# Gated linear attention and two MLPs on one core: plain float32 prefix sums, a state split by head, a guard behind the exponential, twelve weight pieces converted early

## The chip, the cores and the metric

The kernel runs on one core of a Trainium2 chip. TensorE (PE, its weight loads shown as PEld), VectorE (DVE), ScalarE (ACT) and GpSimd (POOL) each work through a queue of their own in program order, and SyncE (SP) issues every DMA. The metric is the device time of one execution in microseconds (us). Lower is better.

## The reference

For 4 batches of 8 heads, 768 tokens and a head size of 48, a gated linear attention runs over the tokens, with a forget gate for each of the 48 rows of the state:

```python
f = 1.0 / (1.0 + np.exp(-f_logit))
for t in range(S):
    state = f[:, :, t, :, None] * state + np.einsum('bhd,bhe->bhde', k[:, :, t], v[:, :, t])
    y[:, :, t] = np.einsum('bhd,bhde->bhe', q[:, :, t], state)
```

Its output x (768 tokens by 384 channels per batch) goes through a token mixing of rank 32 and an MLP, then through a second MLP with a convolution of width 3 over the tokens and a gate:

```python
u = x + (x.T @ U @ V).T
x = u + np.maximum(u @ w_ch1, 0) @ w_ch2          # 384 -> 1536 -> 384
h = np.maximum(x @ w_in, 0)                       # 384 -> 1024
c = conv3(h, conv_w)
out = (h / (1 + np.exp(-c))) @ w_out              # 1024 -> 384
```

The weights arrive as float64, and the kernel turns them into float32 itself.

## The kernel before

**Attention in chunks.** The 768 tokens of a batch are cut into 6 chunks of 128, 24 chunks in all, done one after the other by a loop over `i` (L786 to L858). With the running sum n of log(1 + exp(-f_logit)) inside a chunk, q is scaled by exp(-n) and k by exp(n); then the chunk's own part is a masked product of the two, and what comes from earlier chunks is q times a state of 48 x 48 per head. For chunk g the steps are, by the names in the code:

- `gate_max` (L436, tile sp): the lowest logit is cut off, on POOL from chunk 4 on. `gates` (L441): ACT takes exp (L443) and ln (L444) of sp. From chunk 3 on the result is then split in two float32r parts, the high one sph by ACT (L451), the rest spl by POOL (`sub`, L70).
- `prefix` (L455): the running sum is a matmul with a triangle of ones, once for each part, into the PSUM tile n. ACT makes a = exp(-n) (L467), POOL q times a (tile qh, L473). DVE cuts n off at 64 into b (L470), ACT takes exp of b (L476), POOL multiplies k by it (tile kh, L477).
- `ends` and `ends_back` (L500, L503): the last row of a goes to DRAM and comes back as a column, tile ga. `decay` (L507): POOL multiplies a block mask by it (gm, L510).
- `transposes` (L518) of qh and kh on PE, copied by ACT; `scores` (L527), 8 matmuls into two banks s; `mask` (L537), two multiplications by the triangle on DVE, tiles p.
- `state` (L544): k times v for a pair of heads at a time, 4 matmuls of 112 x 96 into bank kv, off-diagonal blocks included; DVE adds the state (wtmp, L558) and multiplies by gm (w, L559), which clears those blocks too.
- `out_chunk` (L581): y from w and qT and from p and v, in 32-column strips that share the array; `out_evac` (L594) copies it into u; `tokens` (L597), `mix_in` (L609), `mix_z` (L619) and `mix_out` (L635) do the token mixing.

Iteration i runs the scores and output of chunk i, the prefix of chunk i+2 and the gates of chunk i+4. Loads are issued on SP two to three iterations ahead into three buffers per tensor, and each waits for the buffer's last reader.

**Weights.** w_ch1 and w_ch2 come in 24 pieces of 384 KB; DVE turns a piece into float32 with five operations (`w64_steps`, L112 to L116), ACT and POOL split it into float32r parts (`split`, L88). N_EARLY = 6 pieces (three pairs, w1 and w2) are converted inside the attention loop, `SLOT` = 3 steps per iteration put ahead of the masks (`slot`, L743). The other 18 are converted two per unit of the first MLP.

**MLPs.** From iteration 22 on `mlps` is advanced. A unit of the first MLP is 18 float32r matmuls up and 18 down, 384 columns each; there are 12 units for each batch, and DVE makes the low part rl of each unit's activations (L200) in the same queue as the conversions.

Of the kernel before, what the change touches and what calls it, by code (L numbers as in the profile page):

```python
# [17 lines left out]
N_EARLY = 6  # L18
SLOT = 3
N_WHOLE = 3  # L20
# [4 lines left out]
EXP_LIMIT = 64.0  # L25
LEAST_NORMAL = float(897 << 20)
# [3 lines left out]
def kernel(  # L30
# [369 lines left out]
    tri_r = gc.tile([128, 128], F32R, name="tri_r")  # L400
# [3 lines left out]
    bmask = gc.tile([128, 1, D2], F32, name="bmask")  # L404
# [12 lines left out]
    sph, spl, bt = {}, {}, {}  # L417
    gms = {}
# [17 lines left out]
    def gate_max(g):  # L436
        sp = spt[g] = ga2.tile([128, H, D], F32, tag="sp", name="sp")
        (nc.vector if g < 4 else nc.gpsimd).tensor_scalar(  # L438
            out=sp, in0=ft.pop(g), scalar1=LEAST_LOGIT, scalar2=None, op0=ALU.max)

    def gates(g):  # L441
        sp = spt.pop(g)
# [3 lines left out]
        if g < N_WHOLE:  # L446
            sph[g] = sp
            return lambda: None
        h_ = ga2.tile([128, H, D], F32R, tag="sph", name="sph")
        l_ = ga2.tile([128, H, D], F32R, tag="spl", name="spl")  # L450
        nc.scalar.copy(out=h_, in_=sp)  # L451
        sph[g], spl[g] = h_, l_
        return lambda: sub(nc.vector if g < 4 else nc.gpsimd, l_, sp, h_.bitcast(F32))

    def prefix(g, between=None):  # L455
        n = bank(6, [128, DM], "n")
        if g >= N_WHOLE:
            mm(n, tri_r, sph.pop(g).rearrange("p h d -> p (h d)"), True, False)
            mm(n, tri_r, spl.pop(g).rearrange("p h d -> p (h d)"), False, True)
        else:  # L460
            mm(n, tri, sph.pop(g).rearrange("p h d -> p (h d)"), True, True)
# [4 lines left out]
        def up():  # L466
            nc.scalar.activation(out=heads(a_t[g % 3]), in_=nv, func=ACTF.Exp, scale=-1.0)  # L467

        def down():
            nc.vector.tensor_scalar(out=b_, in0=nv, scalar1=EXP_LIMIT, scalar2=None, op0=ALU.min)  # L470

        def q_hat():
            eng.tensor_tensor(out=heads(q_t[g % 2]), in0=qt.pop(g), in1=heads(a_t[g % 3]), op=ALU.mult)  # L473
# [5 lines left out]
        if g < 3:  # L479
            down()  # L480
            up()
            nc.scalar.activation(out=b_, in_=b_, func=ACTF.Exp)
            if between:
                between()
            q_hat()
            eng.tensor_tensor(out=heads(k_t[g % 3]), in0=kt.pop(g), in1=b_, op=ALU.mult)
            return None, None
        up()
        q_hat()
        return down, k_hat  # L490

# [15 lines left out]
    def decay(g):  # L507
        if (g + 1) % NCH:
            gm = wk1.tile([MP, NP, D2], F32, tag="gm", name="gm")
            nc.gpsimd.tensor_tensor(  # L510
                out=gm, in0=bmask[0:MP].to_broadcast([MP, NP, D2]),
                in1=ga[0:MP, g, :].unsqueeze(2).to_broadcast([MP, NP, D2]), op=ALU.mult,
            )
            gms[g] = gm

    qT, kT, sc, pt, wt = {}, {}, {}, {}, {}
# [26 lines left out]

    def state(g):  # L544
        if (g + 1) % NCH == 0:
            return lambda: None
        kh, vv = k_t[g % 3], vt[g]
        ps = bank(7, [MP, NP, D2], "kv")
        for p in range(NP):
            vp = vv[:, p * 128:p * 128 + 2 * VO].rearrange("p (j x) -> p j x", j=2)[:, :, 0:D]  # L550
            mm(ps[:, p, :], kh[:, p, 0:MP], vp, True, True)

        def rest():
            w = wk2.tile([MP, NP, D2], F32, tag="w", name="w")
            gm = gms.pop(g)
            if g % NCH:
                tmp = wk1.tile([MP, NP, D2], F32, tag="wtmp", name="wtmp")
                nc.vector.tensor_tensor(out=tmp, in0=ps, in1=wt[g], op=ALU.add)  # L558
                nc.vector.tensor_tensor(out=w, in0=tmp, in1=gm, op=ALU.mult)  # L559
            else:  # L560
                nc.vector.tensor_tensor(out=w, in0=ps, in1=gm, op=ALU.mult)
            wt[g + 1] = w

        return rest
# [3 lines left out]
    def groups(g, ps, parts, first):  # L568
        started = set() if first else set(range(4))
        rounds = [[] for _ in range(4)]  # L570
        for part in parts:
            rounds[part[0] % 4].append(part)
        while any(rounds):
            for q in rounds:
                if q:
                    gr, lhsT, rhs = q.pop(0)
                    m, c = divmod(gr, 4)
                    mm(ps[32 * c:32 * (c + 1), m, :], lhsT, rhs, c not in started, False)
                    started.add(c)

    def out_chunk(g):  # L581
        yt[g] = ps = bank(4, [128, KD, C], "y")
        qq, vv, pp = qT.pop(g), vt.pop(g), pt.pop(g)
        parts = []
        if g % NCH:
            w = wt.pop(g)
            parts += [(3 * p + x, w[:, p, 32 * x:32 * (x + 1)], qq[:, p, :]) for p in range(NP) for x in range(3)]
        for x, gr, j in ((0, 0, 0), (1, 1, 0), (2, 1, 1), (3, 2, 1)):
            parts += [(3 * p + gr, vv[:, 128 * p + 32 * x:128 * p + 32 * (x + 1)], pp[j][:, p, :]) for p in range(NP)]
        groups(g, ps, parts, True)  # L590
# [28 lines left out]
    def mix_z(b):  # L619
        z = zps.pop(b)  # L620
        lo = wk1.tile([R, DM], F32, tag="zt", name="zt")
        zz = wk1.tile([R, DM], F32, tag="zz", name="zz")
        st = wk1.tile([3 * R, DM], F32R, tag="zst", name="zst")
        nc.scalar.copy(out=lo, in_=z[R:2 * R])
        nc.vector.tensor_tensor(out=zz, in0=z[0:R], in1=lo, op=ALU.add)
# [49 lines left out]
    with tc.manual_schedule():  # L675
# [6 lines left out]
        nc.gpsimd.memset(bmask, 1.0)  # L682
        nc.gpsimd.affine_select(
            out=bmask[:, 0, 0:D], in_=bmask[:, 0, 0:D], pattern=[[0, D]], base=D - 1,
            channel_multiplier=-1, compare_op=ALU.is_ge, fill=0.0,
        )
        nc.gpsimd.affine_select(
            out=bmask[:, 0, D:D2], in_=bmask[:, 0, D:D2], pattern=[[0, D]], base=-64,
            channel_multiplier=1, compare_op=ALU.is_ge, fill=0.0,
        )  # L690
# [5 lines left out]
        nc.vector.tensor_copy(out=tri_r, in_=tri)  # L696
        for t in v_t:
            nc.gpsimd.memset(t[:, 0:NP * 128].rearrange("p (a x) -> p a x", a=NP)[:, :, D:VO], 0.0)
        for t, x in ((q_t[1], 0.0), (k_t[1], 0.0), (a_t[1], 1.0), (k_t[2], 0.0), (a_t[2], 1.0)):
            nc.gpsimd.memset(t, x)  # L700
# [9 lines left out]
        prefix(0, lambda: gate_max(1))  # L710
        warm(WARM_UP[1])
        gate_low = gates(1)
        transposes(0)
        gate_low()
# [58 lines left out]
        slot(5)
        gate_low()
# [10 lines left out]
        lows = []  # L785
        for i in range(1, NG):  # L786
            for g in ((i + 3,) if i == 1 else (5, 6) if i == 2 else (i + 4,)):
                if g < NG:
                    load(kt, k, "k", g)
                    load(qt, q, "q", g)  # L790
            for g in ((5, 6) if i == 1 else (i + 5,)):
                if g < NG:
                    load(ft, f_logit, "f", g)
# [4 lines left out]
            if i > 1:  # L798
                decay(i)
            for low in lows:  # L800
                low()
            lows.clear()
# [13 lines left out]
            if down:  # L816
                down()
# [3 lines left out]
            if i == 1:  # L821
                decay(1)
            state(i)()
# [4 lines left out]
            for g in ((i + 3,) if i == 1 else (5, 6) if i == 2 else (i + 4,)):  # L828
                if g < NG:
                    gate_max(g)  # L830
                    lows.append(gates(g))
            if i == 1:
                lows.pop()()
# [8 lines left out]
            elif (i - 1) % NCH > 1:  # L842
                for at in (1, 7) if i % 2 else (1,):
# [195 lines left out]
```

## Time and profile before

| what | before |
|---|---|
| median of 3 runs | 700.9 us (700.42 to 701.51) |
| the profiled execution, its own time | 703.99 us |
| its span, first to last instruction | 702.3 us |
| granted TensorE clock over the span | 0.987 |
| busy, share of the span: PE, DVE, ACT, POOL | 94%, 66%, 41%, 26% |
| first matmul of the first MLP | at 182.1 us |
| chain that ended last: PE, DVE, POOL, DMA | 66%, 11%, 7%, 5% |

The busy shares are averages over two stages: until 182 us the attention, where four engines and the DMA queues take turns, and after it the MLPs, where PE hardly pauses. A matmul record overlaps the next, so a busy PE of 94% is no measure of its speed; the distance from start to start is. Parts of the text below call the distance between the scores of two successive chunks an interval.

### The profile page before, as it was taken

Reading aid. Unit: us, or ns where it says so; the run is one execution under the profiler, and the core shown is the slowest. Engines: PE = TensorE matmul, PEld = TensorE weight load, DVE = VectorE, ACT = ScalarE, POOL = GpSimd, SP = SyncE. Lnnn points to the kernel's source line nnn. Section 1 sums busy time; section 2 is a strip of 40 time slices with the busy share of each in tenths; the row PEclk is TensorE's granted clock in tenths of the full one; section 3 lists DMA queues with packets and bytes.
Section 4 is the critical chain, followed back from the end, with each engine's and each line's share of the span. In section 5 each row is a group of like instructions: output and inputs, shape, how many; then the busy total and the mean of one; then the engine's idle time right before and its main releaser. Section 6 shows DMA issues by size and latency. Waiting matters only on the chain.

```text
span 702.3 us, 12589 instructions
## 1 busy us (share of the span) xinstructions
PE 657.2 (94%) x5084; PEld 626.8 (89%) x5084; DVE 460.5 (66%) x717; ACT 290.5 (41%) x571; POOL 185.2 (26%) x189
## 2 busy tenths in 40 slices
PE   7788798888999999999999999999999999999994
PEld 6676677777898989999999999999999999999994
DVE  5756786867699999666911141113898769769762
ACT  5567676676422232222311131113454544544532
POOL 4667777784133341111300020002002002002000
PEclk9989999999999999999999999999999999999998
DMA  9868576751033322222000000000000100100102
GB/s 175 160 122 158 116 154 141 151 98 50 2 112 113 113 91 68 68 68 68 23 0 1 1 1 1 0 1 1 1 1 0 69 1 1 67 1 1 69 0 73
DMA packets 126919, 41.13 MB, mean 59 GB/s; under 512 B 113300, under 2 KB 124076, under 8 KB 126852
## 3 DMA queue, kind: packets, MB, share of 16 engines
q1 hardware_dynamic: 126852, 40.24, 24.5%
q8 instruction: 42, 0.69, 0.4%
q14 instruction: 25, 0.20, 0.1%
HBM read 35.46 MB, written 4.77 MB: 57 GB/s over the span
## 4 chain that ended last, share of the span: by engine, by line
PE 66%; DVE 11%; POOL 7%; DMA 5%; issue 4%; ACT 4%; SPq 1%; POOLq 0%; DVEq 0%; ACTq 0%
PE a L67 31%; PE b L67 30%; POOL sp L438 2%; POOL kh L477 2%; DVE cvt L112 2%; DVE cvt L113 2%; DVE cvt L114 1%; DMA f<-in_f_logit_dram 1%; DVE cvg L116 1%; DVE cvg L115 1%; POOL spl L70 1%; PE y L67 1%; DVE ul L70 1%; POOL qh L473 1%; DMA ga<-ends_d 1%
## 5 line engine op out<-in xcount | busy, mean ns | idle before, releaser
L196 ACT ACTIVATE rh<-a 128x384 fp32r<-128x384 f32 x96 | 47.3, 492 | 211.1 <-PE a L67 211.1
L200 DVE SCALAR_TENSOR_TENSOR rl<-a,rh 128x384 fp32r<-128x384 f32 x96 | 52.1, 555 | 123.9 <-ACT rh L196 123.6
L70 POOL TENSOR_TENSOR ul<-u,uh 128x384 fp32r<-128x384 f32 x24 | 29.4, 1253 | 281.7 <-ACT uh L89 272.2
L67 PE MATMUL a<-uh,w1h 128*128 128x384 f32 x288 | 97.0, 337 | 3.3 <-ACT w2h L89 3.3
L67 PE MATMUL a<-ul,w1h 128*128 128x384 f32 x288 | 96.7, 336 | 0.0
L67 PE MATMUL b<-rh,w2h 128*128 128x384 f32 x288 | 96.5, 335 | 0.0
L67 PE MATMUL b<-rh,w2l 128*128 128x384 f32 x288 | 96.3, 334 | 0.0
L67 PE MATMUL a<-uh,w1l 128*128 128x384 f32 x288 | 96.3, 334 | 0.0
L67 PE MATMUL b<-rl,w2h 128*128 128x384 f32 x288 | 96.3, 334 | 0.0
L67 PE MATMUL b<-woh,w1h 128*128 128x384 f32 x264 | 70.9, 337 | 0.0
L67 PE MATMUL a<-ul,winh 128*128 128x384 f32 x192 | 65.3, 340 | 2.2 <-DVE ul L70 2.2
L67 PE MATMUL a<-uh,winh 128*128 128x384 f32 x192 | 64.5, 336 | 0.0
L67 PE MATMUL a<-uh,winl 128*128 128x384 f32 x192 | 64.4, 335 | 0.0
L67 PEld LDWEIGHTS a<-uh,w1h 128*128 128x128 f32 x288 | 54.1, 188 | 5.3 <-ACT w2h L89 5.3
L250 ACT ACTIVATE c<-c 128x768 f32<-128x768 f32 x31 | 26.3, 848 | 68.9 <-DVE c L280 68.8
L67 PEld LDWEIGHTS a<-ul,w1h 128*128 128x128 f32 x288 | 54.1, 188 | 0.6 <-DVE ul L70 0.6
L67 PEld LDWEIGHTS b<-rh,w2h 128*128 128x128 f32 x288 | 54.1, 188 | 0.4 <-issue 0.3
L67 PEld LDWEIGHTS b<-rl,w2h 128*128 128x128 f32 x288 | 54.1, 188 | 0.0
L67 PEld LDWEIGHTS a<-uh,w1l 128*128 128x128 f32 x288 | 54.1, 188 | 0.0
L67 PEld LDWEIGHTS b<-rh,w2l 128*128 128x128 f32 x288 | 54.1, 188 | 0.0
L67 PEld LDWEIGHTS b<-woh,w1h 128*128 128x128 f32 x264 | 48.1, 188 | 0.0
L67 PE MATMUL b<-wol,w1h 128*128 128x384 f32 x132 | 44.4, 336 | 0.0
(133 smaller groups left out, 1357.1 us busy)
## 6 DMA issues: line engine op xcount, KB each, us to landing
raw<-in_moe_w_ch_dram SPq DMA_DIRECT2D x24, 384.0 KB
f<-in_f_logit_dram SPq DMA_DIRECT2D x24, 192.0 KB
k<-in_k_dram SPq DMA_DIRECT2D x24, 192.0 KB
q<-in_q_dram SPq DMA_DIRECT2D x24, 192.0 KB
v<-in_v_dram SPq DMA_DIRECT2D x48, 96.0 KB
out_dram<-o SPq DMA_DIRECT2D x24, 192.0 KB
raw<-in_moe_w_in_dram SPq DMA_DIRECT2D x8, 384.0 KB
raw<-in_moe_w_out_dram SPq DMA_DIRECT2D x8, 384.0 KB
```

Source lines behind the costliest of these rows:

```text
L67: nc.tensor.matmul(out=out, lhsT=lhsT, rhs=rhs, start=start, stop=stop, skip_group_check=True)
L70: eng.tensor_tensor(out=out, in0=a, in1=b, op=ALU.subtract)
L112: lambda: ve.tensor_scalar(out=t, in0=hi, scalar1=3, scalar2=0x3FFFFFFF, op0=ALU.logical_shift_left, op1=ALU.bitwise_and),
L113: lambda: ve.scalar_tensor_tensor(out=t, in0=hi, scalar=-(1 << 30), in1=t, op0=ALU.bitwise_and, op1=ALU.bitwise_or),
L114: lambda: ve.scalar_tensor_tensor(out=t, in0=lo, scalar=29, in1=t, op0=ALU.logical_shift_right, op1=ALU.bitwise_or),
L115: lambda: ve.tensor_scalar(out=g, in0=hi, scalar1=0x7FF00000, scalar2=None, op0=ALU.bitwise_and),
L116: lambda: ve.scalar_tensor_tensor(out=w, in0=g, scalar=LEAST_NORMAL, in1=t.bitcast(F32), op0=ALU.is_ge, op1=ALU.mult),
L196: nc.scalar.activation(out=rh[:, hf], in_=ps, func=ACTF.Relu)
L200: nc.vector.scalar_tensor_tensor(out=rl[:, hf], in0=ps, scalar=0.0, in1=rh[:, hf].bitcast(F32), op0=ALU.max, op1=ALU.subtract,)
L250: nc.scalar.activation(out=c, in_=c, func=ACTF.Sigmoid)
L438: (nc.vector if g < 4 else nc.gpsimd).tensor_scalar(out=sp, in0=ft.pop(g), scalar1=LEAST_LOGIT, scalar2=None, op0=ALU.max)
L477: eng.tensor_tensor(out=heads(k_t[g % 3]), in0=kt.pop(g), in1=b_, op=ALU.mult)
```

## The change

- **Prefix sums in plain float32.** The split of sp (L451, L70) is gone, and one float32 matmul with `tri` replaces the two of float32r, for every chunk.
- **Guard behind the exponential.** ACT takes exp(n) straight from PSUM; the cut-off (min and max in one two-operator instruction) is then made on b in SBUF, by POOL from chunk 2 on. DVE's cut-off of n is gone. `gate_max` on POOL also becomes a two-operator instruction, min with 3.0e38 and max with the lowest logit.
- **Block-diagonal state, updated in the next chunk.** k times v is made in strips of 32 rows for each head by itself (16 matmuls of 32 x 48), behind y of the chunk. In the next iteration DVE adds the state (two operations of 48 x 192) and POOL multiplies by ga (two more). gm and the block mask are gone.
- **Order.** From iteration 4 on `gates(i + 3)` stands ahead of the prefix instead of `gates(i + 4)` at the iteration's end, and `gate_max(i + 4)` at its end. Loads of k and q are issued for chunk i+3, of f for i+4.
- **Twelve weight pieces** in the attention, five steps per iteration (3 ahead of the masks, 2 at the end). `mix_z` copies both halves of z out by ACT; `mix_out` uses other banks.

```diff
-N_EARLY = 6
-SLOT = 3
+N_EARLY = 12
+SLOT = (3, 2)
+EARLY_GATES = 4
...
     def gate_max(g):
-        (nc.vector if g < 4 else nc.gpsimd).tensor_scalar(
-            out=sp, in0=ft.pop(g), scalar1=LEAST_LOGIT, scalar2=None, op0=ALU.max)
+        if g < 4:
+            nc.vector.tensor_scalar(out=sp, in0=ft.pop(g), scalar1=LEAST_LOGIT, scalar2=None, op0=ALU.max)
+        else:
+            nc.gpsimd.tensor_scalar(
+                out=sp, in0=ft.pop(g), scalar1=LARGEST, scalar2=LEAST_LOGIT, op0=ALU.min, op1=ALU.max)
...
-            mm(n, tri_r, sph.pop(g).rearrange("p h d -> p (h d)"), True, False)
-            mm(n, tri_r, spl.pop(g).rearrange("p h d -> p (h d)"), False, True)
+        mm(n, tri, sps.pop(g).rearrange("p h d -> p (h d)"), True, True)
...
         def k_hat():
-            nc.scalar.activation(out=b_, in_=b_, func=ACTF.Exp)
+            nc.scalar.activation(out=b_, in_=nv, func=ACTF.Exp)
+            eng.tensor_scalar(
+                out=b_, in0=b_, scalar1=exp(EXP_LIMIT), scalar2=0.0, op0=ALU.min, op1=ALU.max)
             eng.tensor_tensor(out=heads(k_t[g % 3]), in0=kt.pop(g), in1=b_, op=ALU.mult)
...
     def state(g):
...
+        kvs[g] = ps = bank(7, [128, NP, D], "kv")
...
         for p in range(NP):
+            for x in range(4):
+                e = p * 128 + (x // 2) * VO
+                parts.append((x, ps[32 * x:32 * (x + 1), p, :], kh[:, p, 32 * x:32 * (x + 1)], vv[:, e:e + D]))
+    def state_end(g):
...
             if g % NCH:
...
+                nc.vector.tensor_tensor(out=tmp[r], in0=ps[r], in1=w_t[g % 2][r, :, cs], op=ALU.add)
+                nc.gpsimd.tensor_tensor(out=w[r, :, cs], in0=tmp[r], in1=end, op=ALU.mult)
...
             out_evac(i - 1)
             scores(i)
+            if i % NCH:
+                state_end(i - 1)
+            if EARLY_GATES <= i and i + 3 < NG:
+                gates(i + 3)
             follow = slot_end()
             if 1 < i < FILL_FROM:
-                slot(SLOT)
+                slot(SLOT[0])
...
-            state(i)()
...
+            if EARLY_GATES <= i + 1 and i + 4 < NG:
+                gate_max(i + 4)
+            if 1 < i < FILL_FROM:
+                slot(SLOT[1])
```

**POOL, one iteration with a weight piece, before** (spl the low part of the gates, w1l that of a weight piece):

```order
L510 TENSOR_TENSOR gm<-bmask,ga 112x384
L70 TENSOR_TENSOR spl<-sp,sph 128x384
L70 TENSOR_TENSOR w1l<-cvg,w1h 128x3x128
L473 TENSOR_TENSOR qh_113<-q,a_111 128x8x48
L477 TENSOR_TENSOR kh_116<-k,b 128x8x48
L438 TENSOR_SCALAR sp<-f 128x384
```

The same place on POOL in the changed kernel (b is the guard, w_105 the state):

```order
L528 TENSOR_TENSOR w_105<-wtmp,ga 48x4x48 x2
L71 TENSOR_TENSOR w1l<-cvg,w1h 128x3x128
L455 TENSOR_TENSOR qh_113<-q,a_111 128x8x48
L459 TENSOR_SCALAR b<-b 128x384
L461 TENSOR_TENSOR kh_116<-k,b 128x8x48
L440 TENSOR_SCALAR sp<-f 128x384
```

gm and spl have gone, two halves of w and the guard have come; sp still closes the iteration.

**ACT, the same iteration, before**:

```order
L443 ACTIVATE sp<-sp 128x384
L444 ACTIVATE sp<-sp,one 128x384
L451 CAST sph<-sp 128x384
L595 COPY u_68<-y 128x3x128
L89 CAST w1h<-cvg 128x3x128
L467 ACTIVATE a_110<-n 128x8x48
```

ACT in the changed kernel:

```order
L571 COPY u_68<-y 128x3x128
L445 ACTIVATE sp<-sp 128x384
L446 ACTIVATE sp<-sp,one 128x384
L90 CAST w1h<-cvg 128x3x128
L454 ACTIVATE a_110<-n 128x8x48
```

The copy of y, which PE's next transposes wait for, has moved ahead of the gates; the gates' exponential and logarithm still stand ahead of a, which POOL's qh waits for.

**PE, one iteration behind the scores, before**:

```order
L67 MATMUL n<-sph,tri_r 128x384
L67 MATMUL n<-spl,tri_r 128x384
L67 MATMUL z<-xh,uhl 64x384
L67 MATMUL z<-xl,uhl 64x384
L600 MATMUL xt<-ident,u_68 128x128 x3
L67 MATMUL kv<-v_118,kh_115 112x96 x4
L522 MATMUL qTp<-ident,qh_114 112x128 x4
```

PE in the changed kernel, from the same place to the end of the iteration:

```order
L68 MATMUL n<-sp,tri 128x384
L68 MATMUL z<-xh,uhl 64x384
L68 MATMUL z<-xl,uhl 64x384
L576 MATMUL xt<-ident,u_68 128x128 x3
L486 MATMUL qTp<-ident,qh_114 112x128 x4
L486 MATMUL kTp<-ident,kh_117 112x128 x4
L68 MATMUL mix<-vst,zst 128x384
L68 MATMUL y<-qT,w_105 32x128 x12
L68 MATMUL y<-p_1435,v_120 32x128 x8
L68 MATMUL y<-p_1451,v_120 32x128 x8
L68 MATMUL kv<-v_120,kh_116 32x48 x16
```

The prefix is one matmul, and kv has moved from the middle of the iteration to its end.

## Rows read from the trace of the kernel before

**Rows 1.** Stretches (us): PE, PEld, DVE, ACT, POOL busy (count), clock, DMA share, GB/s

```profile
15.68:46.82 31.14, 22.02 (x287) 18.77 (x284) 19.33 (x33) 17.41 (x36) 20.12 (x21) 0.84 0.79 151
46.82:176.36 129.54, 112.41 (x1728) 94.03 (x1724) 97.43 (x167) 89.28 (x184) 93.70 (x90) 0.99 0.62 122
130.68:137.00 6.32, 6.08 (x101) 5.21 (x97) 6.02 (x11) 4.38 (x9) 5.39 (x6) 1.00 0.79 167
170.46:176.36 5.90, 5.66 (x99) 4.84 (x95) 4.43 (x9) 3.27 (x7) 0.00 (x0) 1.00 0.17 65
```

**Rows 2.** Timeline of PE: start, us, scores of chunks 1, 5 and 23

```profile
15.68 1.16 PE L67 MATMUL s<-qT,kT 48*128 48x128 f32 x16
...
52.45 1.16 PE L67 MATMUL s<-qT,kT 48*128 48x128 f32 x16
...
176.36 1.16 PE L67 MATMUL s<-qT,kT 48*128 48x128 f32 x16
```

**Rows 3.** Groups by line and form, 0 to 185 us: busy us, mean ns | idle

```profile
L438 POOL TENSOR_SCALAR sp<-f 128x384 f32<-128x384 f32 x20 | 26.4, 1321 | 0.0
L473 POOL TENSOR_TENSOR qh<-q,a 128x384 f32<-128x384 f32 x22 | 22.3, 1013 | 6.4 <-ACT a L467 5.4 <-POOL spl L70 0.9
L477 POOL TENSOR_TENSOR kh<-k,b 128x384 f32<-128x384 f32 x21 | 21.8, 1038 | 4.9 <-ACT b L476 4.7
L70 POOL TENSOR_TENSOR spl<-sp,sph 128x384 fp32r<-128x384 f32 x20 | 20.0, 1003 | 21.5 <-ACT sph L451 21.5
...
L444 ACT ACTIVATE sp<-sp,one 128x384 f32<-128x384 f32 x24 | 14.8, 616 | 0.8
...
L443 ACT ACTIVATE sp<-sp 128x384 f32<-128x384 f32 x24 | 12.5, 522 | 28.9 <-POOL sp L438 26.2 <-DVE sp L438 2.5
L467 ACT ACTIVATE a<-n 128x384 f32<-128x384 f32 x24 | 11.8, 492 | 9.8 <-PE n L67 6.0 <-DVE b L470 3.8
...
L451 ACT CAST sph<-sp 128x384 fp32r<-128x384 f32 x21 | 10.7, 512 | 0.7
```

**Rows 4.** Waits, 0 to 185 us: us in total, times, longest

```profile
ACT sp L443 <- POOL sp L438: 26.2, 17, 2.5
POOL spl L70 <- ACT sph L451: 21.5, 18, 1.8
POOL gm L510 <- DMA ga<-ends_d: 13.4, 4, 9.6
```

**Rows 5.** Timeline of PE: a plain prefix with its successor, a split one

```profile
13.90 0.84 PE L67 MATMUL n<-sp,tri 128*128 128x384 f32 x2
14.66 1.08 PE L67 MATMUL y<-p,v 128*32 128x128 f32 x32
...
108.31 0.45 PE L67 MATMUL n<-sph,tri_r 128*128 128x384 f32 x1
...
108.76 0.34 PE L67 MATMUL z<-xh,uhl 128*64 128x384 f32 x1
```

**Rows 6.** Other POOL groups by line and form, 0 to 185 us

```profile
L70 POOL TENSOR_TENSOR uhl<-cvg,uhl 128x192 fp32r<-128x192 f32 x1 | 0.6, 598 | 1.9 <-ACT uhl L89 1.9
...
L700 POOL MEMSET kh<- 128x512 f32 x2 | 1.0, 518 | 0.0
```

**Rows 7.** Timeline of DVE: one conversion step beside POOL's w1l, one alone

```profile
117.88 1.24 DVE L114 SCALAR_TENSOR_TENSOR cvt<-raw,cvt 128x384 int32<-128x384 int32 x1
...
193.93 0.56 DVE L114 SCALAR_TENSOR_TENSOR cvt<-raw,cvt 128x384 int32<-128x384 int32 x1
```

**Rows 8.** Chain that ended last: start, us; units with and without conversions

```profile
232.41 0.93 DVE rl L200 x2
...
239.47 0.93 DVE rl L200 x2
...
273.47 3.12 PE a L67 x18
276.59 3.12 PE b L67 x18
```

More of the change, by code (lines that the diff above doesn't have):

```diff
@@ L403 @@
     ends_d = dr.tile([NG, 1, NP * 128], F32, name="ends_d")
-    bmask = gc.tile([128, 1, D2], F32, name="bmask")
+    w_t = [gc.tile([MP, NP, D2], F32, name=f"w{i}") for i in range(2)]
     one = gc.tile([128, 1], F32, name="one")
@@ L416 @@
     ft, qt, kt, vt = {}, {}, {}, {}
-    sph, spl, bt = {}, {}, {}
-    gms = {}
+    sps = {}
     def load(dst, src, nm, g):
@@ L505, in ends_back @@
             nc.sync.dma_start(out=ga[0:MP, g, :], in_=ends_d[g].rearrange("o (p d) -> d (o p)", d=128)[0:MP])
[L507 to L516, printed above, removed]
+    qT, kT, sc, pt = {}, {}, {}, {}
     def transposes(g):
@@ L542, in mask, with strips @@
         pt[g].append(t)
+    kvs = {}
     def state(g):
-        if (g + 1) % NCH == 0:
-            return lambda: None
         kh, vv = k_t[g % 3], vt[g]
-        ps = bank(7, [MP, NP, D2], "kv")
+        kvs[g] = ps = bank(7, [128, NP, D], "kv")
+        parts = []
         for p in range(NP):
[L550 to L555, printed above, removed]
+            for x in range(4):
+                e = p * 128 + (x // 2) * VO
+                parts.append((x, ps[32 * x:32 * (x + 1), p, :], kh[:, p, 32 * x:32 * (x + 1)], vv[:, e:e + D]))
+        return parts
+    def state_end(g):
+        ps, w = kvs.pop(g), w_t[(g + 1) % 2]
+        for j in range(2):
+            r, cs = slice(64 * j, 64 * j + D), slice(j * D, (j + 1) * D)
+            end = ga[r, g, :].unsqueeze(2).to_broadcast([D, NP, D])
             if g % NCH:
-                tmp = wk1.tile([MP, NP, D2], F32, tag="wtmp", name="wtmp")
-                nc.vector.tensor_tensor(out=tmp, in0=ps, in1=wt[g], op=ALU.add)
-                nc.vector.tensor_tensor(out=w, in0=tmp, in1=gm, op=ALU.mult)
-            else:
-                nc.vector.tensor_tensor(out=w, in0=ps, in1=gm, op=ALU.mult)
-            wt[g + 1] = w
-        return rest
+                tmp = wk1.tile([MP, NP, D], F32, tag=f"wtmp{j}", name="wtmp")
+                nc.vector.tensor_tensor(out=tmp[r], in0=ps[r], in1=w_t[g % 2][r, :, cs], op=ALU.add)
+                nc.gpsimd.tensor_tensor(out=w[r, :, cs], in0=tmp[r], in1=end, op=ALU.mult)
+            else:
+                nc.vector.tensor_tensor(out=w[r, :, cs], in0=ps[r], in1=end, op=ALU.mult)
     xh, xl = {}, {}
-    def groups(g, ps, parts, first):
-        started = set() if first else set(range(4))
+    def strips(parts, started):
         rounds = [[] for _ in range(4)]
         for part in parts:
-            rounds[part[0] % 4].append(part)
+            rounds[part[0]].append(part)
         while any(rounds):
@@ L582, in out_chunk, with add @@
         yt[g] = ps = bank(4, [128, KD, C], "y")
-        qq, vv, pp = qT.pop(g), vt.pop(g), pt.pop(g)
+        qq, vv, pp = qT.pop(g), vt[g], pt.pop(g)
         parts = []
+        def add(gr, lhsT, rhs):
+            m, c = divmod(gr, 4)
+            parts.append((c, ps[32 * c:32 * (c + 1), m, :], lhsT, rhs))
         if g % NCH:
-            w = wt.pop(g)
-            parts += [(3 * p + x, w[:, p, 32 * x:32 * (x + 1)], qq[:, p, :]) for p in range(NP) for x in range(3)]
+            w = w_t[g % 2]
+            for p in range(NP):
+                for x in range(3):
+                    add(3 * p + x, w[:, p, 32 * x:32 * (x + 1)], qq[:, p, :])
         for x, gr, j in ((0, 0, 0), (1, 1, 0), (2, 1, 1), (3, 2, 1)):
-            parts += [(3 * p + gr, vv[:, 128 * p + 32 * x:128 * p + 32 * (x + 1)], pp[j][:, p, :]) for p in range(NP)]
-        groups(g, ps, parts, True)
+            for p in range(NP):
+                e = 128 * p + 32 * x
+                add(3 * p + gr, vv[:, e:e + 32], pp[j][:, p, :])
+        strips(parts, set())
+        if (g + 1) % NCH:
+            strips(state(g), set())
+        vt.pop(g)
     yt = {}
@@ L620, in mix_z @@
         z = zps.pop(b)
-        lo = wk1.tile([R, DM], F32, tag="zt", name="zt")
-        zz = wk1.tile([R, DM], F32, tag="zz", name="zz")
+        up, lo, zz = [wk1.tile([R, DM], F32, tag=t, name=t) for t in ("zu", "zt", "zz")]
         st = wk1.tile([3 * R, DM], F32R, tag="zst", name="zst")
+        nc.scalar.copy(out=up, in_=z[0:R])
         nc.scalar.copy(out=lo, in_=z[R:2 * R])
-        nc.vector.tensor_tensor(out=zz, in0=z[0:R], in1=lo, op=ALU.add)
+        nc.vector.tensor_tensor(out=zz, in0=up, in1=lo, op=ALU.add)
         zst[b] = st
@@ L709 @@
         warm(WARM_UP[0])
-        prefix(0, lambda: gate_max(1))
+        k_hat = prefix(0)
+        k_hat()
+        gate_max(1)
         warm(WARM_UP[1])
-        gate_low = gates(1)
+        gates(1)
         transposes(0)
-        gate_low()
         gate_max(2)
@@ L759 @@
         stage()
-        prefix(1)
-        decay(0)
+        prefix(1)()
         scores(0)
-        gate_low = gates(2)
+        gates(2)
         mask(0, 0)
         mask(0, 1)
-        gate_low()
         gate_max(3)
         transposes(1)
-        state_dve = state(0)
-        prefix(2, state_dve)
-        gate_low = gates(3)
+        prefix(2)()
+        gates(3)
         slot(5)
-        gate_low()
         out_chunk(0)
@@ L784 @@
         slot(1)
-        lows = []
         for i in range(1, NG):
[L787 to L793, printed above, removed]
+            if i + 3 < NG:
+                load(kt, k, "k", i + 3)
+                load(qt, q, "q", i + 3)
+            if i + 4 < NG:
+                load(ft, f_logit, "f", i + 4)
             if i + 3 < NG:
@@ L827 @@
                 transposes(i + 1)
[L828 to L833, printed above, removed]
+            if i < EARLY_GATES:
+                gate_max(i + 3)
+                gates(i + 3)
+            if EARLY_GATES <= i + 1 and i + 4 < NG:
+                gate_max(i + 4)
+            if 1 < i < FILL_FROM:
+                slot(SLOT[1])
             if i + 2 < NG:
```

72 lines of the change are left out of this document (12 added, 60 removed).

## Prediction

> **What bounds the kernel now.** I read the stretches first, then the starts of the scores, the groups by line, the waits, and last the chain. From 46.82 us to 176.36 us no engine is full: of 129.54 us PE is busy 112.4, DVE 97.4, POOL 93.7, ACT 89.3, and the DMA share is 0.62 [rows 1]. Where the gates are already done, one chunk takes 5.90 us with PE busy 5.66; over the whole attention the 18 intervals from chunk 5 (52.45) to chunk 23 (176.36) take 123.9 us, 6.88 each, and the four from chunk 1 (15.68) to chunk 5 take 36.8, 9.2 each [rows 2]. So a chain through several engines sets the pace, and the waits name it: ACT's exponential waits for POOL's sp 17 times, 26.2 us in all, and POOL's spl for ACT's sph 18 times, 21.5 us [rows 4].
>
> That chain is a ring: sp on POOL 1.32, exp 0.52, ln 0.62 and sph 0.51 on ACT, then spl 1.00, qh 1.01 and kh 1.04 on POOL, and the next sp stands behind kh in POOL's queue [rows 3]. The sum is 6.02; with some 0.3 for seven hand-offs it is 6.3, the length of the interval that ends at 137.00 [rows 1]. The work of PE comes close behind it.
>
> In the first MLP a unit with two conversions takes 239.47 - 232.41 = 7.06 us, one without takes 3.12 + 3.12 = 6.24 [rows 8]: there DVE, with the conversions and rl in one queue, sets the pace.
>
> **The change part by part.**
>
> *The ring.* sph and spl leave it. But POOL still ends an iteration with sp, ACT still has exp and ln ahead of a, and qh still waits for a: so a ring is left, sp, exp, ln, a 0.49, qh, guard, kh. It goes round once per chunk, as before. What it costs hangs on the two-operator instruction, which sp and the guard both become. No row shows one on POOL. The nearest is the one-operator sp, 1.32 us on average [rows 3]; a memset of 128x512, with no input, takes 0.52 [rows 6]; and if each operator had to be paid for, it would be about 2.0. Oddly the one-input sp takes longer than qh with two inputs of the same size, 1.01. So reading is not what limits sp, and another form may well be quicker. I take 0.8, below qh, as it reads half as much, and keep 0.5 and 2.0 as ends. The ring is then 0.8 + 0.52 + 0.62 + 0.49 + 1.01 + 0.8 + 1.04 + 0.3 = 5.6. In an iteration with a weight piece, ACT's w1h (about the 0.51 of sph) stands ahead of a, and POOL's w1l (about the 1.00 of spl) ahead of qh, covering a: 5.6 - 0.49 + 0.51 + 1.00 = 6.6. With 12 pieces that happens 12 times.
>
> By the Trainium skill's page "GPSIMD Engine Reference", section "Engine selection", a one-input elementwise operation runs on GpSimd at roughly line rate. The 1.32 us of sp disagree for one operator; no row here shows two. By that page the price would be an estimated 0.5, which is the first rival below.
>
> *PE.* A plain prefix takes 14.66 - 13.90 = 0.76, the split pair 108.76 - 108.31 = 0.45 [rows 5]: 0.31 more per chunk. kv as 16 strips: the strips of y are the nearest, 32 matmul records from 14.66 to 15.68, 1.02 us for 16 matmuls of 128 moving columns [rows 2, 5]; here there are 48 columns, so from 0.4 to 1.0, and I take 0.85, about what kv costs now. The chunk without a prefix has 5.66 of PE work [rows 1]; with 0.76 it is 6.4 where a token-mixing matmul runs beside it, about 6.05 where none does, and a chunk in six needs no state and another no kv. I take 6.2 as PE's floor. So in the 12 iterations with a piece the ring's 6.6 holds, rounded up to 6.7 for DVE's port (below), elsewhere PE's 6.2.
>
> *Intervals 5 to 23.* 12 x 6.7 + 4 x 6.2 + 2 x 5.8 (the last two, without gates) = 116.8 against 123.9: **-7.1 us**.
>
> *The head, chunks 1 to 5.* Here gm waits for the state's decay, which goes through DRAM: 13.4 us in 4 waits [rows 4]. In the changed kernel ga is needed a chunk later, which hides it. Until iteration 4 the gates stay at the end, and n waits for ln, so the ring gains the prefix: 5.6 + 0.76 = 6.4, about 6.5. The last of the four has two sp, 7.3. 3 x 6.5 + 7.3 = 26.8 against 36.8, less 0.7 because in chunk 0 DVE's cut-off now comes behind ACT's exponential and delays the next gates: **-9.3 us**. The granted clock, 0.84 in this stretch [rows 1], may rise with shorter gaps; I count nothing for it, and 3 us in the range.
>
> *DVE and POOL.* DVE loses the cut-off of n and the product w, and gains the steps of six pieces. POOL loses gm and spl, and gains two halves of w (0.60 each, from the 128x192 uhl [rows 6]), the guard and six w1l. Both halves of w lie beside ACT's exp, ln and a. Steps of DVE and work of POOL slow each other: L114 takes 1.24 beside w1l and 0.56 alone [rows 7]. That is the 0.1 above.
>
> *DMA.* Twelve pieces instead of six add 2.3 MB to the stage, while its share is 0.62 [rows 1]; loads are issued an iteration later than before, but still a whole iteration ahead of use. Nothing, as long as the queue does not fall behind.
>
> *MLP.* Nine units had two conversions, six will have: 3 x (7.06 - 6.24) = **-2.5 us**. The rest of the kernel is untouched.
>
> *Sum.* -7.1 - 9.3 - 2.5 = -18.9. The profiled execution takes 703.99 us; 685.1. The median of the runs is 3.1 below that execution: **682.0 us**.
>
> **The rivals.**
>
> 1. *The two-operator form is quick, 0.5.* The ring drops under PE in all iterations, 6.0 with a piece. Then 16 x 6.3 + 2 x 5.8 = 112.4 (-11.5), head 3 x 6.1 + 6.5 = 24.8 (-11.3), MLP -2.5: 25.3 less, 675.6. For it speaks that sp is slower than an instruction with twice the input; against it, that no row shows such an instruction.
> 2. *It costs what one operator costs, 1.27 to 1.32.* The ring is 1.0 longer: 7.6 with a piece, 6.6 without. 12 x 7.6 + 4 x 6.6 + 11.6 = 129.2 (+5.3), head 3 x 7.5 + 8.7 = 31.2 (-4.9), MLP -2.5: 2 less, about 699. For it: it is the nearest row.
> 3. *Slower: each operator is paid for, 2.0.* Two instructions of the ring are 1.2 longer each: 12 x 9.1 + 4 x 8.0 + 11.6 = 152.8 (+28.9), head 3 x 8.9 + 12 = 38.7 (+2.6), MLP -2.5: 29 more, 730. The point from which the change loses is a price of about 1.35. Against it: max alone is no more work than the product in qh, so its 1.32 holds more than the arithmetic.
> 4. *DVE and POOL take turns.* If a step of DVE with two inputs and an instruction of POOL never ran together, an iteration with a piece would take POOL's 2 x 0.6 + 1.0 + 1.01 + 0.8 + 1.04 + 0.8 = 5.9 and five steps of about 0.48, 2.4: 8.3. That is 12 x 1.6 = 19 us more than the forecast, 701. The interval up to 137.00 speaks against it: POOL's six instructions and DVE's four that could collide come to about 8.0 uncontended, and it took 6.32 with POOL busy 5.39 and DVE 6.02 [rows 1]. The Trainium skill's page "SBUF — State Buffer", section "SBUF: two separate sides", says of this port pair that whichever of the two engines starts first gets it for the whole instruction and the other fully blocks. By that rule this rival holds; rows 7 agree for a single step, that interval does not for the whole.
> 5. *The plan does not take hold*: f lands late, and ACT waits as before. The ring then keeps its 26 us of waits; the head and the MLP still gain, 11.8 us: 689.
>
> **How the numbers follow.** Forecast 0.48 (a price from 0.6 to 1.1, 676 to 692), first rival 0.24, second 0.11, third 0.05, fourth 0.07, fifth 0.05. About 0.2%, 1.4 us, is what a measurement can tell from no change. Faster: all of the forecast, the first and the fifth, and half of the second and the fourth, 0.86; slower: the third and a part of the second and the fourth, 0.10; the rest, 0.04, the same. The range goes from 672 (the first rival with the better clock) to 698, which leaves out the third, most of the fourth and some of the second.
>
> **What would show it.** In the changed profile: POOL's sp and b near 0.8; ACT's wait for sp below 10 us in all; intervals of 6.2 to 6.7 from chunk 5 on, and chunk 5's scores near 43 us; the first matmul of the MLP near 166; n at 0.76; units of 6.24 from about 7 units into the MLP. Wrong: sp or b above 1.3; an idle PE waiting for qh or kh in each interval; steps of DVE that all take a microsecond; f landing behind its use.

## The result, and the profile after

The changed kernel takes **682.68 us** (median of 4 runs, 680.04 to 684.42), the kernel before beside it 700.66: ratio 0.974, 95% interval [0.9704, 0.9777]. The forecast was 682.0. The profiled execution of the changed kernel took 680.04 us, with a span of 678.3; its first MLP matmul starts at 165.40 us.

The stretches from chunk 1 to chunk 5 and from chunk 5 to chunk 23 (the view of [rows 1]), then the interval of chunk 3 with its two halves; columns as in [rows 1]:

```profile
17.64:48.34 30.70, 23.41 (x482) 20.16 (x475) 18.86 (x36) 17.34 (x38) 18.62 (x27) 0.94 0.79 154
48.34:159.53 111.19, 101.26 (x1995) 84.34 (x1988) 95.06 (x172) 78.51 (x169) 79.89 (x103) 1.00 0.77 160
...
30.17:42.38 12.21, 7.00 (x127) 6.14 (x120) 4.29 (x9) 5.17 (x11) 5.06 (x8) 0.86 0.85 168
32.00:37.20 5.20, 2.24 (x15) 1.60 (x14) 1.20 (x3) 2.92 (x7) 3.14 (x4) 1.00 0.72 151
37.20:42.40 5.20, 3.40 (x90) 3.37 (x90) 2.38 (x5) 0.86 (x3) 0.57 (x1) 0.67 0.89 167
```

And the starts of the scores of chunks 1, 3, 4 and 23 on PE (the view of [rows 2]):

```profile
17.64 1.16 PE L68 MATMUL s<-qT,kT 48*128 48x128 f32 x16
...
30.17 1.16 PE L68 MATMUL s<-qT,kT 48*128 48x128 f32 x16
42.38 1.16 PE L68 MATMUL s<-qT,kT 48*128 48x128 f32 x16
...
159.53 1.16 PE L68 MATMUL s<-qT,kT 48*128 48x128 f32 x16
```

So the span is shorter by 702.3 - 678.3 = 24.0 us. Chunk 1 starts 1.96 later (15.68 to 17.64). Chunk 1 to chunk 5 takes 30.70 for 36.77: -6.07. Chunk 5 to chunk 23 takes 111.19 for 123.91: -12.72, or 6.18 us an interval. From chunk 23 to the MLP it is 5.87 for 5.78. The MLP takes 512.9 for 520.1: -7.2. Of the 24.0, 18.0 are in the medians; the rest is that the profiled execution of before lies 3.3 above the median now taken beside it, and that of after 2.6 below its own. A second profile of the changed kernel (changed_again, below) has 32.78 for the head and 111.07 from chunk 5 to 23: the second stretch repeats, the head varies by some 2 us.

From 48.34 to 159.53 us PE is now busy 101.26 of 111.19 (91%), DVE 95.06 (85%), POOL 79.89, ACT 78.51; while conversions run (48 to 143 us) DVE is at 90% and the DMA engines at 0.87. No engine is full, but three are near it.

POOL's groups by line and form from 0 to 170 us (the view of [rows 3]):

```profile
L461 POOL TENSOR_TENSOR kh<-k,b 128x384 f32<-128x384 f32 x22 | 23.4, 1064 | 1.8
L455 POOL TENSOR_TENSOR qh<-q,a 128x384 f32<-128x384 f32 x22 | 22.3, 1014 | 23.1 <-DVE cvt L114 11.7 <-ACT a L454 3.9 <-POOL w L528 3.8
L528 POOL TENSOR_TENSOR w<-wtmp,ga 48x192 f32<-48x192 f32 x32 | 16.7, 522 | 14.6 <-DVE wtmp L527 13.3
L459 POOL TENSOR_SCALAR b<-b 128x384 f32<-128x384 f32 x22 | 13.3, 605 | 1.9
L440 POOL TENSOR_SCALAR sp<-f 128x384 f32<-128x384 f32 x20 | 12.4, 621 | 2.7 <-DMA v<-in_v_dram 2.7
```

The clamp sp took 1.32 us with one operator and takes 0.62 with two; the guard b takes 0.605. The waits from 0 to 170 us (the view of [rows 4]; us in total, times, longest):

```profile
POOL w L528 <- DVE wtmp L527: 13.3, 10, 4.3
DVE wtmp L527 <- PE kv L68: 12.0, 10, 3.0
...
ACT sp L445 <- POOL sp L440: 11.5, 14, 2.1
```

ACT's wait for sp fell from 26.2 to 11.5 us, the wait of gm for the row of chunk ends is gone with gm.

### The profile page after: what moved, and what is told of

Read it like the earlier page. It is cut to its first block, busy times and chain, and to the rows that moved or that the text cites. A ratio compares the mean times of both kernels' runs of the same rounds, so it can differ in the third digit from the quotient of the medians.

```text
span 678.3 us, 13514 instructions
## 1 busy us (share of the span) xinstructions
PE 647.8 (95%) x5564; PEld 620.4 (91%) x5564; DVE 441.2 (65%) x697; ACT 278.0 (41%) x554; POOL 164.7 (24%) x202
## 4 chain that ended last, share of the span: by engine, by line
PE 79%; DVE 7%; ACT 4%; POOL 3%; issue 3%; DMA 2%; SPq 1%; DVEq 0%; POOLq 0%; ACTq 0%
PE a L68 37%; PE b L68 36%; PE y L68 3%; DVE ul L71 1%; DMA q<-in_q_dram 1%; POOL qh L455 1%; PE n L68 1%; PE s L68 1%; DVE p L503 1%; DVE xl L71 1%; PE kv L68 1%; ACT a L454 1%; DVE wtmp L527 1%; ACT xh L579 1%; ACT sp L445 1%
```

## The experiments

Each run was timed beside the kernel before on its chip. Ratios are to that; where a text turns a difference of two ratios into microseconds, it takes it times 702.

**Is the two-operator form what carries it?** First the clamp, then the guard too, back in one operator:

```
-  sp: scalar1=LARGEST, scalar2=LEAST_LOGIT, op0=min, op1=max
+  sp: scalar1=LEAST_LOGIT, scalar2=None, op0=max
   (one_op_both also:)
-  b:  scalar1=exp(EXP_LIMIT), scalar2=0.0, op0=min, op1=max
+  b:  scalar1=exp(EXP_LIMIT), scalar2=None, op0=min
```

> The changed kernel with GpSimd's clamp of the gate logits back in its one-operator form (maximum alone); everything else as changed. By the rows that form took 1.32 us in the kernel before and the two-operator form 0.62 us after: 0.70 us more on GpSimd for each of 20 chunks. Theory A, the prediction's ring (GpSimd and ScalarE hand one chunk round, so every microsecond on GpSimd is on the path): intervals from 6.2 to 6.9 us, total up by 12 to 14 us, near 696 us. Theory B (after the change no engine carries alone: GpSimd is busy 4.9 of 6.2 us an interval and has 1.3 us free): total up by less than 4 us, under 687 us.

> The changed kernel with both the clamp and the guard on GpSimd in their one-operator forms, which is the prediction's second rival (699 us, ratio 0.995 to 0.997): if one operator takes 1.19 us as in the run with the clamp alone, GpSimd does 1.2 us more for a chunk than in the changed kernel. Theory A (every microsecond on GpSimd's round is paid at the same rate as for the clamp, 10 to 12 us for the first 0.6): another 9 to 12 us, 704 to 707 us, so that the two-operator form decides whether the change gains at all. Theory B (the guard stands behind the products that TensorE waits for, and has slack that the clamp has not): under 5 us more than the clamp alone, 695 to 700 us.

Measured: 694.87 us, ratio 0.9885 [0.9851, 0.9918], for the clamp alone; 703.26 us, ratio 1.0031 [1.0011, 1.0052], for both. Here is the clamp on POOL from 48 to 160 us, in the changed kernel and in the first of these runs; the three numbers are the least, median and largest duration in ns:

```profile
L440 POOL TENSOR_SCALAR sp<-f x16: 498/577/823, 48.2 to 141.1; 128x384 f32<-128x384 f32 x16
```

```profile
L440 POOL TENSOR_SCALAR sp<-f x16: 1157/1186/1472, 50.0 to 152.8; 128x384 f32<-128x384 f32 x16
```

Same tile, same data, one operator fewer, twice the time. In the run with both, the guard takes 1.30 and the wait for sp is back:

```profile
L459 POOL TENSOR_SCALAR b<-b 128x384 f32<-128x384 f32 x22 | 28.7, 1304 | 2.4 <-ACT b L458 0.6
L440 POOL TENSOR_SCALAR sp<-f 128x384 f32<-128x384 f32 x20 | 25.7, 1286 | 0.0
```

```profile
ACT sp L445 <- POOL sp L440: 38.4, 19, 4.1
```

The clamp costs 0.0145 x 702 = 10 us for 0.66 more in each of 20 chunks, 0.77 for every microsecond on POOL; the guard another 10 for 0.70 in each of 22, 0.66. For the clamp that is near theory A's range and far from B's; the guard's further 10 us are what A gave. Without the two-operator form the change would be no gain at all: its sign hung on a price that no row of before showed.

**Does the order of the gates matter?** All gates at the end of the iteration, so that a chunk's clamp, exponential and logarithm must be through before the next iteration's prefix:

```
-EARLY_GATES = 4
+EARLY_GATES = 21
```

> The changed kernel with the gates of a chunk (clamp, exponential, logarithm) at the end of the iteration for all chunks, as in the iterations 1 to 3, instead of clamped at the end of one iteration and taken through ScalarE at the start of the next. Theory A (the ring is what the interval is made of: clamp 0.62, exponential 0.52 and logarithm 0.62 us come back into the wait of one chunk): ScalarE's wait for the clamp goes from 6 us to over 15 us, intervals to 6.6 to 7 us, total near 690 to 697 us. Theory B (there is a chunk of slack either way): total within 2 us of 682.7 us.

Measured: 701.39 us, ratio 0.9982 [0.9963, 1.0001]. No instruction differs, and it takes 17 us more than the changed kernel; even more than theory A gave. The waits from 0 to 185 us show the ring:

```profile
ACT sp L445 <- POOL sp L440: 38.9, 20, 3.0
POOL w L528 <- DVE wtmp L527: 30.3, 14, 7.4
PE y L68 <- DVE xl L71: 18.4, 14, 5.2
PEld n L68 <- ACT sp L446: 15.9, 17, 1.6
```

Now the prefix waits 15.9 us for the logarithm, 3.4 in the changed kernel. The intervals from chunk 5 to 23 come to 126.00 us, 7.0 each. This order is not that of before: there the gates of a chunk stood at the end of the iteration two ahead of the one with its prefix, here they stand at the end of the iteration just ahead of it. So the run shows what that lead is worth, which the kernel before had too. What the change's own reordering gave was not measured by itself.

**What do the parts give alone?** The kernel before with the plain prefix for all chunks, then with the two-operator clamp too:

```
-N_WHOLE = 3
+N_WHOLE = 24
   (before_whole_two also:)
-  sp: scalar1=LEAST_LOGIT, scalar2=None, op0=max
+  sp: scalar1=3.0e38, scalar2=LEAST_LOGIT, op0=min, op1=max
```

> The kernel before with one part of the change alone: every chunk's prefix sum as one plain float32 matmul, as its first three chunks have it, without the hi and lo parts. It takes a copy (0.51 us on ScalarE) and a subtraction (1.00 us on GpSimd) from each of 21 chunks and adds 0.31 us on TensorE. Theory A (GpSimd's time is the path, and the one-operator clamp put back into the changed kernel cost 10 to 12 us for 0.61 us more in each of 20 chunks, about 0.9 us for every microsecond): down by 15 to 20 us, ratio 0.971 to 0.979. Theory B (GpSimd's microsecond goes into its wait for the row of chunk ends in front of the mask product, 13.4 us in all before, and the interval hardly moves): down by less than 5 us, ratio over 0.993.

> The kernel before with the plain prefix sums and the two-operator clamp, but the state, the guard and the weight pieces as before. Against the run with the plain prefix alone it takes another 0.6 to 0.7 us from GpSimd in each of 20 chunks. Theory A (GpSimd on the path): another 10 to 12 us less, so that these two parts give nearly all of the change's 18 us, ratio 0.957 to 0.975. Theory B (what follows is held by the row of chunk ends and the state's masks): less than 4 us below the run with the plain prefix alone; what the whole change gives beyond that comes from the state and the pieces.

Measured: 692.73 us, ratio 0.9874 [0.9837, 0.9912]; and 689.36 us, ratio 0.9814 [0.9776, 0.9853]. That is 8.8 us for the prefix, between the two theories, and about 4 more for the clamp: theory B's end, though the intervals of the two runs touch. The order of before gives part of what POOL gains to another wait; in the second of these runs (0 to 175 us):

```profile
POOL qh L473 <- DMA q<-in_q_dram: 17.1, 8, 3.5
ACT sp L443 <- POOL sp L438: 16.0, 18, 3.1
POOL gm L510 <- DMA ga<-ends_d: 14.0, 5, 12.1
```

ACT's wait for sp went from 26.2 to 16.0, but POOL now waits 17.1 us for q and still 14.0 for the row of chunk ends. In the changed kernel the row is used a chunk later by w, off this path. So some 0.6 us on POOL was worth about 4 us in the old kernel and 10 in the new; which of the new order, state and guard makes the difference was not taken apart. These three, with the smaller edits of `mix_z` and `mix_out`, bring about another 4 us (0.9814 to the 0.9756 of the next run, which has six pieces as these two; the intervals overlap).

**Are the twelve pieces worth anything?**

```
-N_EARLY = 12
-SLOT = (3, 2)
+N_EARLY = 6
+SLOT = (3, 0)
```

> The changed kernel with six weight pieces in the attention instead of twelve, and three conversion slots an iteration instead of five, as before the change. Theory A (the six pieces cost the attention little, since its intervals stand at TensorE's own work, and the gain of 7.5 us in the MLP is theirs): chunk 5 to chunk 23 stays within 2 us of 111.2 us, the MLP takes 520 us instead of 512.7, total near 689 us. Theory B (VectorE at 91% and the DMA engines at 88% hold the intervals too): chunk 5 to chunk 23 falls to 103 to 107 us and the total stays within 3 us of the changed kernel's 682.7 us.

Measured: 684.96 us, ratio 0.9756 [0.9725, 0.9788]; chunk 5 to 23 in 109.90 us, the MLP in 515.3. Each theory has half: the attention hardly moves, as A says, and the total stays, as B says, since the MLP pays 2.4 us and not 7. Between 0.974 and 0.9756 these runs tell nothing apart: twelve pieces or six, it is about the same.

**What sets the head?** The interval from chunk 3 to chunk 4 takes 12.21 us. The chain of the changed kernel there (start, us):

```profile
31.09 1.41 SPq L478
...
33.59 2.22 DMA raw<-in_moe_V_dram
...
35.94 0.37 DVE cvt L113
...
36.33 0.74 DVE cvt L114
...
37.10 1.29 DVE p L503 x2
38.38 0.48 DVE xl L71
...
39.00 3.15 PE y L68 x56
```

SyncE comes to the load of V's second half only at 32.59, behind the chunk's own loads; DVE waits 4.8 us for it in front of the masks p; y waits for DVE, and then takes 3.15 us in place of the 1.73 of the chunk before (at 28.16 us): the granted clock is 0.67 in that stretch, a mean over its two levels, 2.4 and 1.2 GHz, after a stretch in which PE was busy 2.24 of 5.20 us. Two runs:

```
v_early:     v_ld = load_v(1) at the start of iteration 2
head_light:  load v two chunks ahead instead of three;
             slots from iteration 4 instead of 2; N_EARLY = 10
```

> The changed kernel with the load of V's second half issued at the start of iteration 2, ahead of that iteration's k, q, f and v, instead of behind them. Theory A (the 4.8 us that VectorE waits for this load in front of the masks of chunk 3 are on the path): the interval from chunk 3's scores to chunk 4's falls from 12.2 to about 7.5 us, first MLP matmul near 161 us, total down by 4 to 5 us, near 678 us. Theory B (SyncE's queue and the DMA engines are full in the head, so that whatever is issued earlier makes the chunk's own loads as much later): the 12.2 us are only spread over chunks 4 to 7, total within 1.5 us of 682.7 us.

> The changed kernel with less loaded in the first iterations: v two chunks ahead instead of three, conversion slots from iteration 4 instead of 2, ten pieces in the attention. Before chunk 5's scores fall V's second half, a weight piece and one chunk's v, 0.88 MB, which at the 180 GB/s of these slices are 4.9 us. Theory A (the head is set by the DMA engines, which is why the earlier load of V's second half only spread its 5 us): chunk 5's scores from 48.3 to 43 to 45 us, first MLP matmul 3 to 5 us earlier, total down by 2 to 4 us after two pieces more in the MLP. Theory B (the head is set by the ring, the 12.2 us interval by the order of the queue on VectorE): chunk 5's scores within 1.5 us of 48.3 us.

Measured: v_early 682.69 us, ratio 0.9729 [0.9689, 0.9769]: nothing. The three intervals from chunk 2 to chunk 5 take 7.50, 7.63 and 9.69 for 6.63, 12.21 and 5.96, the same 24.8 us: theory B. POOL waits there for q (3.2 us) and DVE for the convolution's weights (2.6).

head_light: 684.59 us, ratio 0.9748 [0.9714, 0.9782]. Its head is what theory A gave, chunk 5 at 43.09 us; but from there to chunk 23:

```profile
43.09:161.95 118.86, 102.86 (x1995) 86.05 (x1988) 96.15 (x170) 78.68 (x169) 78.42 (x100) 0.99 0.74 150
```

118.86 us for 111.19, with each engine busy about as long as in the changed kernel. The 5 us were won and given back. A weight piece is six conversion steps on DVE, five of them run in an iteration, which makes five pieces in the six chunks of a batch: each chunk of a batch always has the same steps. My reading: starting ten steps later moved these against the chunk at which the batch's low-rank product comes, and twelve would not. The next run tests that, with the changed kernel itself beside it:

```
head_phase:  as head_light, and no second slots in iteration 4 (12 steps later)
```

> The changed kernel itself, beside the next two on the same chip: ratio 0.974 within 0.003.

> As head_light, but with twelve conversion steps left out at the start instead of ten (none in iterations 2 and 3, three in iteration 4). A piece has six steps, so the pieces again meet the batch's low-rank product at the same step as in the changed kernel. Theory A (head_light lost its 5 us again because ten steps shifted that meeting): chunk 5's scores near 43 us as there, chunk 5 to chunk 23 back from 118.9 to 111 to 113 us, first MLP matmul near 161 us, total 678 to 680 us. Theory B (with the head shorter, or v loaded later, something else takes the time back, such as a transfer or VectorE's backlog): chunk 5 to chunk 23 over 116 us again, total 683 to 686 us.

Measured: the changed kernel again 684.3 us, ratio 0.9753 [0.9735, 0.9771]; **head_phase 678.79 us, ratio 0.967 [0.9651, 0.9689]**. Chunk 5 and chunk 23 there:

```profile
43.70 1.16 PE L68 MATMUL s<-qT,kT 48*128 48x128 f32 x16
...
156.96 1.16 PE L68 MATMUL s<-qT,kT 48*128 48x128 f32 x16
```

113.26 us between them: 0.3 above theory A's range and far from B's, and the total is A's; the MLP starts at 162.83 (161 expected). Two steps more left out are the only difference to head_light; what exactly collides at the other meeting was not taken apart. That the head is set by what is loaded and not by the conversion steps themselves rests on v_early and on the loads that its waits name; head_light left out both. With less of either, the head takes 26.18 (head_light) and 26.06 us (head_phase) from chunk 1 to chunk 5.

**PE's wait for the tokens.** The transposed tokens share a PSUM bank with the outputs, so y waits for DVE's xl:

```
-  tokens: ps = bank(4, ...)      mix_out in banks 7, 6, before out_chunk
+  tokens: ps = bank(7, ...)      mix_out in banks 1, 0, behind out_chunk
   (combo: head_phase with this edit, up to iteration 21)
```

> The changed kernel with the transposed tokens in the PSUM bank of the state sums instead of the bank of the chunk's outputs, and the low-rank products behind the outputs in the two banks of the transposes. TensorE's outputs then no longer wait for VectorE's subtraction that reads the tokens (8 us in 112 us named so, 0.14 to 0.9 us each). Theory A (TensorE at 91% and this wait are the interval): down by 5 to 9 us, intervals near 5.8 us. Theory B (the interval is the ring over GpSimd, ScalarE and VectorE, and TensorE's wait only moves): within 2 us of 682.7 us.

> As head_phase, and the tokens in the bank of the state sums with the low-rank products behind the outputs as in xt_bank, but both in their old banks from iteration 22 on, so that the MLP's first matmul finds its banks free. Theory A: xt_bank was 0.9 us ahead at chunk 23 and lost 3.5 us behind it to the banks of the MLP, so here 1 to 3 us come on top of head_phase, total 676 to 679 us. Theory B (TensorE's wait for the tokens only moves): within 1 us of head_phase.

Measured: xt_bank 683.13 us, ratio 0.9724 [0.9689, 0.9759]: theory B, 111.32 us from chunk 5 to 23. The wait for xl went, and ACT's wait for sp came in its place (24.6 us between 50 and 160 us). combo, with the old banks at the end, 677.72 us, ratio 0.9661 [0.9636, 0.9686]: not to be told from head_phase. Both beat the changed kernel, by some 0.8 to 0.9%, and the kernel before by 3.3 to 3.4%.

## Why the prediction came out right, and where it was wrong

The median was met (682.0 for 682.68), and the mechanism is borne out, but three terms were off by about 5 us each. Their errors partly cancelled, and the pair of profiles differs by 6 us more than the medians do: that the forecast came within 0.7 us is luck.

- *The ring* as what sets the pace: right. One microsecond on POOL a chunk was worth 0.66 to 0.77 (one_op_max, one_op_both), and the same instructions in another order lost 17 us (late_gates). The term that was mis-sized is **the price of the two-operator instruction**: 0.8 was taken, 0.62 and 0.605 measured. The forecast's reason, that max alone at 1.32 was too dear for what it reads, was the right one; it was not followed far enough. The break-even price of 1.35 was close: with 1.29 and 1.30 the ratio is 1.0031. The second rival, 699 for that price, was 4 us too kind. The Trainium skill's page "GPSIMD Engine Reference", section "Engine selection", has a one-input operation run at roughly line rate, by which the prediction estimated 0.5. The quickest two-operator clamp, 0.50 us, agrees; the one-operator form, never under 1.16, does not.
- *Intervals 5 to 23*: -7.1 forecast, -12.7 measured. With the price of 0.5 the first rival had 112.4 us for this stretch; it took 111.19. With the measured prices the forecast's own ring comes to 5.2 us, 6.2 with a weight piece, and PE is busy 5.6 of 6.18 an interval: both now lie close together, which fits that a microsecond on POOL is no longer worth a whole one. *PE*: the plain prefix was right, 80.55 to 81.65 us from n to the tokens, 1.10, for 0.79 between the same points before (0.31 more). **kv strips** were too dear at 0.85; they take 0.48, from 96.47 to the next scores at 96.95:

```profile
96.47 0.55 PE L68 MATMUL kv<-v,kh 128*32 128x48 f32 x32
96.95 1.16 PE L68 MATMUL s<-qT,kT 48*128 48x128 f32 x16
```

- *The head, chunks 1 to 5*: -9.3 forecast with the late start, -4.1 measured (30.70 + 1.96 for 36.77). **The step that failed is that it was costed as a ring alone.** The row of chunk ends was hidden as foreseen; behind it stood the loads. With fewer loads and conversion steps there, head_light and head_phase took 26.2 and 26.1 us, near the 26.8 of the forecast's ring. In the changed kernel the DMA engines are busy at 0.77 to 0.90 in every slice of 12 us up to 48 us, SyncE's queue is hardly ever empty from 14 to 41 us, and one conversion stands ahead of the masks in DVE's queue. The stated trust that loads come "a whole iteration ahead of use" was wrong for V. Chunk 1 came 1.96 later, not 0.7. Of that 1.03 us lie in DVE's first clamp, which took 2.02 us instead of 0.65 and ended at 5.58 instead of 4.55, 0.22 us after the last of POOL's memsets; behind it DVE's guard, kh and the next chunk's cut-off now all stand behind ACT's second exponential.
- *DVE and POOL*: the halves of w take 0.52 each (0.60 forecast). The fourth rival falls as a time (701 for the measured 682.68, 8.3 us an interval with a piece for some 6.2), but what it supposes of the two engines holds. A conversion step with two inputs in SBUF takes 0.56 us alone; beside POOL it waits, and POOL for it (the profile after):

```profile
92.79 0.56 DVE L117 SCALAR_TENSOR_TENSOR cvg<-cvg,cvt 128x384 f32<-128x384 int32 x1
...
100.55 1.01 POOL L455 TENSOR_TENSOR qh<-q,a 128x384 f32<-128x384 f32 x1
100.99 0.98 DVE L117 SCALAR_TENSOR_TENSOR cvg<-cvg,cvt 128x384 f32<-128x384 int32 x1
101.64 0.70 POOL L459 TENSOR_SCALAR b<-b 128x384 f32<-128x384 f32 x1
```

  qh ends at 101.56 and the step 0.41 us later, at 101.97; b, which began at 101.64 while the step still ran, takes 0.70 instead of 0.51. From 48 to 160 us all 23 such steps that began while a POOL instruction ran ended 0.41 to 0.42 us after it. The Trainium skill's page "SBUF — State Buffer", section "SBUF: two separate sides", has whichever starts first, a GpSimd instruction or a DVE operation with two SBUF inputs, block the other for the whole instruction; the trace agrees for these steps. The interval up to 137.00, which the prediction held against the rule, does not speak against it: in the profile before, the step at its start waited for gm too, and ended 0.42 us after it.

```profile
130.09 0.93 POOL L510 TENSOR_TENSOR gm<-bmask,ga 112x384 f32<-112x384 f32 x1
130.37 1.07 DVE L113 SCALAR_TENSOR_TENSOR cvt<-raw,cvt 128x384 int32<-128x384 int32 x1
```

  The rival was too dear because it added all of POOL's time to all conversion steps. A step waits only for the rest of one instruction, and operations that read PSUM pay nothing: two masks p take 1.29 us beside POOL and without it. In all, the 36 two-input steps wait some 6 us of the 111, the 24 one-input ones some 4 (0.35 alone, 0.53 on average). Such waiting counts as busy time, so the busy times of DVE (95.06) and POOL (79.89) added up cannot settle whether the two took turns.
- *DMA, nothing*: wrong for the head; in the steady stretch the margin was thin (0.62 before, 0.87 now up to 143 us), but with six pieces fewer the stretch is only 1.3 us shorter (six_pieces).
- *MLP*: -2.5 forecast, -7.2 in the two profiles. The prediction counted nine slow units in before, one for each with two conversions; its trace has six, of about 7.05 us. There are none in the profiled execution after (-5.0 with what lies around them), but one in the run of the changed kernel again and two in v_early. six_pieces, which has as many conversions left for the MLP as before, has two, and no variant of the changed kernel has more. So **the number of pieces, by which the prediction went, does not explain them**; before_whole has five and before_whole_two four with the MLP's code untouched. What sets their number stays open. Another 2.2 us lie behind the last unit's start, 24.6 before and 22.4 after; other runs with the same code there have 22.4 to 24.4, so that is not shown to be an effect of the change.

Against its own profiled execution the forecast was 685.1, and 680.04 came. The forecast was 5 us too slow: 5.6 in the intervals and 4.7 in the MLP, less 5.2 by which the head was forecast too fast.

## What to carry to other kernels

When a loop's engines hand one item round, look at the order first: taking the gates' lead of one iteration away cost 17 us here, nearly as much as the whole change gave. Time one unknown instruction form before a change hangs on it, since here the sign did. Busy time can hold waiting for another engine, so look at single instructions before adding busy times up. And shortening one stretch can shift how periodic side work meets the main loop; check the stretch behind it before calling the saving lost.

## What the runs showed of the hardware

- On POOL a clamp of 128x384 float32 in SBUF takes 1.28 us with max alone and 0.62 with min and max (means; the least 1.16 and 0.50); the guard, min alone and min with max, 1.30 and 0.605.
- The granted clock was 0.67 in the 5.2 us that followed 5.2 us with PE busy 2.24, and the y matmuls of one chunk took 3.15 us instead of 1.73 there: the stall of PE cost more than its own length. In head_light it was 0.59 (67.0 to 71.2 us) after 7.0 us with PE busy 5.09. Both clocks are means over stretches with both levels, 2.4 and 1.2 GHz.
- A DVE step of 128x384 with two inputs in SBUF took 0.56 us alone and, begun beside a POOL instruction, ended 0.41 to 0.42 us after that one (up to 1.26 us); DVE operations with an input in PSUM took the same beside POOL as alone.
- The state sums, 16 matmuls of 48 columns in 32-column strips of PE, take 0.48 us from their start to that of the next matmul.
